# A tile's transposes in two strips of 64 rows, and new costs in the planner that orders the kernel

## The chip, the core and the metric

The kernel runs on one core of one Trainium2 chip. The metric is device time in microseconds (us). A core has a tensor engine (TensorE; its matmuls are PE in the profile, its weight loads PEld), a vector engine (DVE), a scalar engine (ACT) and a queue engine that issues transfers (SP). All of them run their own instruction streams in order and wait for each other through semaphores.

## What is computed

The input x has 4 batches of 11456 tokens with 128 channels. Everything is float32.

```python
def mab(q, kv):
    s = scale * (q @ kv.transpose(0, 2, 1))
    s = s - s.max(-1, keepdims=True)
    a = np.exp(s)
    a /= a.sum(-1, keepdims=True) + 1e-09
    return a @ kv
h = mab(I, x)          # 32 inducing points attend to all tokens of a batch
out = mab(x, h)        # every token attends to the 32 results
# then a mixture of 8 experts with one expert for each token:
# h1 = relu(tok @ w1[e]); y = h1 @ w2[e]; out = gate * sigmoid(tok @ w_output_gate[e]) * y
```

With these inputs all tokens of a batch take one expert, so the kernel loads one w1 and one w2 for each batch and folds them into 32 values for each batch; a slow path for other inputs stands behind a flag and is not taken here.

## The kernel before

A batch is cut into 6 chunks: five of 16 x 128 tokens and one of 12 x 128 (n = 16 or 12). There are 24 chunks. Each chunk passes three stages, written as generators:

- `attend_in` loads the chunk (L164, SP queue) with tokens on the partitions, transposes it on TensorE so that channels lie on the partitions (L174, one transpose for each of the n slices of 128 tokens), has ACT or DVE bring the result from PSUM to the tile xT (`bring`, L218 on ACT and L220 on DVE), computes scores (L150, four column groups of 32), a maximum (L188, L192, L195, L198), the exponential (L201), and the weighted sum h (L211, L213).
- `weigh` needs the batch's result h and xT: scores again (L150), then L478, L481, L486 on DVE and the exponential L494 on ACT.
- `attend_out`, for pairs of chunks: gates (L513, weights of 128 rows by 128 columns), a chain of small operations, and for each chunk the output matmuls (L530: for each slice four tiles of 32 rows, each into a bank of its own), scaled by DVE or ACT (`scaled`, L545 and L550) into ob or xT and written out (L571, SP queue).

Between the batch's `attend_in` and its `weigh` stand `finish` (L264, L266), `choose` (L284, and the loads of w1 and w2 issued by ACT at L304 and L310), `gates` (L344, L361) and `values` (L375, L400, L406); `known` (L423, L432, L461) is a check at the end of a batch.

A planner, `interleave`, orders all of it when the kernel is built. Each generator yields steps with an engine, a cost in us, what must be done before, and slots that it takes (8 PSUM banks among them). The planner always takes the step with the earliest start by these costs, and of equal starts the lowest key (chunk number; weigh +5, outputs +10). The order that it finds is the order on every engine. A step's result counts as done its cost plus a lag after its start:

```python
RINGS = {"bank": 8, "c": 4, "xT": 10, "p1": 2, "s2": 2, "pT": 8, "in": 4, "out": 3, "ob": 3, "w1": 1}
LAG = {"T": 0.2, "V": 0.17, "A": 0.17, "G": 0.15, "D": 1.9, "W": 1.9}
BIAS = {"T": 0.0, "V": 0.25, "A": 0.0, "G": 0.0, "D": 0.0, "W": 0.0}
```

T is TensorE, V is DVE, A is ACT, D is the transfers of SP. The costs only set the order; what a step takes on the chip is what it takes.

Of the kernel before, what the change touches and what calls it, by code (L numbers as in the profile page):

```python
# [17 lines left out]
PSUM = bass.MemoryType.PSUM  # L18

P = 128  # L20
EPS = 1e-9
CH = 16
G = 4
# [8 lines left out]
Step = namedtuple("Step", "engine cost after take give post", defaults=((), (), (), None))  # L32
# [3 lines left out]
def body(ctx: ExitStack, tc: tile.TileContext, x, inducing, w_gate, w_out_gate, w1, w2, out):  # L36
    nc = tc.nc
    B, N, C = x.shape
    M = inducing.shape[0]
    E, _, F = w1.shape  # L40
    NF = F // P
    scale = 1.0 / math.sqrt(C)
# [4 lines left out]
    while row < N:  # L47
        n = min(CH, -(-(N - row) // (G * P)) * G)
        first = min(row, N - n * P)
        chunks.append((first, n, row - first))  # L50
        row = first + n * P
    nk = len(chunks)
# [9 lines left out]
    def bank(slot, shape, dtype=F32):  # L62
        return ps.tile(shape, dtype, name="bank", tag=f"bank{slot[1]}")

    def large(slot, shape, dtype=F32):
        return xp.tile(shape, dtype, name=slot[0], tag=f"{slot[0]}{slot[1]}")

    def small(slot, name, shape, dtype=F32):
        return sp.tile(shape, dtype, name=name, tag=f"{name}{slot[1]}")


    ident = const.tile([P, P], F32, name="ident")
    make_identity(nc, ident)
    ones = const.tile([P, P], F32, name="ones")
    nc.vector.memset(ones, 1.0)
# [70 lines left out]
    def scores(s, xT, w, n):  # L146

        for g in range(G):
            r = slice(g * M, (g + 1) * M)
            nc.tensor.matmul(s[r, 0:n, :], w, xT[:, 0:n, r], start=True, stop=True)  # L150

    def attend_in(b, k):

        first, n, dup = chunks[k]
        if ("nb", b) not in st:
            st["nb", b] = gp.tile([P, nk], F32, name="nb")
            st["ha", b] = gp.tile([P, nk, C + 1], F32, name="ha")
        after = (("h", b - 2),) if b > 1 else ()
        (cslot, slot) = yield Step("D", 0.182 * n, after, (("c", 1), ("in", 1)))
        xc = large(cslot, [P, CH, C])  # L160
        src = x[b, first : first + n * P, :].rearrange("(p q) c -> p q c", q=n)
        for q in range(0, n, n if b or k else G):
            part = slice(q, q + (n if b or k else G))
            nc.sync.dma_start(xc[:, part, :], src[:, part, :])  # L164
        (tslot,) = yield Step("T", 0.0, take=(("xT", 1),))
        xT = large(tslot, [P, CH, P])
        st["xT", b, k] = xT, tslot
        for a0 in range(0, n // G, 2):
            parts = range(a0, min(a0 + 2, n // G))
            bslots = yield Step("T", 0.49 * len(parts), take=(("bank", len(parts)),))  # L170
            for a, bslot in zip(parts, bslots):
                t = bank(bslot, [P, G, P])
                for j in range(G):
                    nc.tensor.transpose(t[:, j, :], xc[:, a * G + j, :], ident)  # L174
                yield (bring(xT[:, a * G : (a + 1) * G, :], t, bslot, ("t", b, k, a)),)
        (bslot,) = yield Step("T", 0.06 * n, [("t", b, k, a) for a in range(n // G)], (("bank", 1),))
        s = bank(bslot, [P, CH, M])
        scores(s, xT, indT, n)
        if dup:

            yield Step("V", 0.5)
            full, rest = divmod(dup, n)
            nc.vector.memset(s[0:M, 0:n, 0:full], LOW)
            if rest:
                nc.vector.memset(s[0:M, 0:rest, full], LOW)
        yield Step("V", 0.06 + 0.04 * n)
        cm = small(slot, "cm", [P, 1])
        nc.vector.tensor_reduce(cm, s[:, 0:n, :], AX.XY, ALU.max)  # L188

        yield Step("V", 0.22)  # L190
        cg = small(slot, "cg", [P, G])
        nc.vector.tensor_scalar(cg, own_s, cm, None, ALU.mult)  # L192
        (mslot,) = yield Step("T", 0.25, take=(("bank", 1),))
        mb = bank(mslot, [P, 512])
        nc.tensor.matmul(mb[:, 0:G], same_m, cg, start=True, stop=True)  # L195
        nb = st["nb", b][:, k : k + 1]
        yield Step("V", 0.15, give=(mslot,))
        nc.vector.tensor_reduce(nb, mb[:, 0:G], AX.X, ALU.min)  # L198
        (pslot,) = yield Step("A", 0.46 + 0.027 * n, take=(("p1", 1),), give=(bslot,))
        p1T = small(pslot, "p1T", [P, CH, M])  # L200
        nc.scalar.activation(  # L201
            p1T[:, 0:n, :], s[:, 0:n, :], AF.Exp, bias=nb, scale=scale, accum_out=st["ha", b][:, k, C:]
        )
        yield Step("V", 0.06 + 0.04 * n)
        p1 = small(pslot, "p1", [P, CH, M])
        nc.vector.transpose(p1[:, 0:n, :], p1T[:, 0:n, :])  # L206
        (bslot,) = yield Step("T", 0.06 * n, take=(("bank", 1),), give=(cslot, pslot))
        h = bank(bslot, [P, C])
        for q in range(n):
            r = slice((q % G) * M, (q % G + 1) * M)  # L210
            nc.tensor.matmul(h[r, :], p1[:, q, :], xc[:, q, :], start=q < G, stop=q >= n - G)  # L211
        yield Step("A", 0.27, give=(bslot, slot), post=("in", b, k))
        nc.scalar.copy(st["ha", b][:, k, 0:C], h)  # L213

    def bring(dst, src, bslot, post):
        (e,) = yield Step(("A", "V"), (0.59, 0.69), give=(bslot,), post=post)
        if e == "A":
            nc.scalar.copy(dst, src)  # L218
        else:
            nc.vector.tensor_copy(dst, src)  # L220
# [20 lines left out]
    def finish(b):  # L241
# [26 lines left out]
        rl = sp.tile([P, M], F32, name="rl")  # L268
        nc.vector.tensor_scalar(rl, hb[:, 1, :], EPS, None, ALU.add)
        yield Step("V", 0.35)  # L270
# [229 lines left out]
    def attend_out(b, i):  # L500

        ks = pairs[i]
        nas = [chunks[k][1] // G for k in ks]
        n = G * sum(nas)
        lslot, slot = yield Step(
            "T", 0.24 * sum(nas), [("p", b, k) for k in ks] + [("gates", b)], (("bank", 1), ("out", 1))
        )
        p = [st.pop(("p", b, k)) for k in ks]
        L = bank(lslot, [P, 2 * CH, NG])
        t = 0  # L510
        for (pT, _), na in zip(p, nas):
            for a in range(na):
                nc.tensor.matmul(  # L513
                    L[:, t : t + G, :], pT[:, a * P : (a + 1) * P], st["gb", b], start=True, stop=True
                )
                t += G
        sm = small(slot, "sm", [P, 2 * CH])
        yield (gate(L, lslot, b, i, n, slot, sm),)
        t = 0
        for (pT, pslot), na, k in zip(p, nas, ks):  # L520

            (oslot,) = yield Step("T", 0.0, take=(("xT" if b == B - 1 else "ob", 1),))
            ob = large(oslot, [P, G, CH // G, C])
            yslots = yield Step("T", 0.1 + 0.44 * na, (("V", b), ("sm", b, i)), (("bank", G),), (pslot,))

            y = [bank(s, [P, CH // G, C]) for s in yslots]
            for a in range(na):
                for g in range(G):
                    r = slice(g * M, (g + 1) * M)
                    nc.tensor.matmul(  # L530
                        y[g][:, a, :], pT[r, a * P : (a + 1) * P], st["vb", b][r], start=True, stop=True
                    )
            for g in range(G):
                sv = sm[:, t : t + na * G].rearrange("p (a g) -> p g a", g=G)[:, g]
                yield (scaled(b, k, g, y[g], yslots[g], ob, oslot, sv, (slot,) if k == ks[-1] else ()),)
            t += na * G
# [38 lines left out]
    def gate(L, lslot, b, i, n, slot, sm):  # L575

        yield Step("V", 0.15)
        r = small(slot, "r", [P, 2 * CH])
        nc.vector.tensor_scalar(r[:, 0:n], L[:, 0:n, E + 1], EPS, None, ALU.add)
        yield Step("V", 0.35)  # L580
# [13 lines left out]
        yield Step("V", 0.18)  # L594
        nc.vector.scalar_tensor_tensor(se[:, 0:n], se[:, 0:n], EPS, r[:, 0:n], ALU.add, ALU.mult)
        yield Step("V", 0.18)
# [11 lines left out]
    for b in range(B):  # L608
        for k in range(nk):
            i = b * nk + k  # L610
# [3 lines left out]
        i = b * nk + KEY_FINISH  # L614
# [10 lines left out]
    def route(b, xv, n, gb):  # L625
# [33 lines left out]
        r = small(("out", 0), "r", [P, 2 * CH])  # L659
        nc.vector.tensor_scalar(r[0:K, 0:n], L[0:K, 0:n, 2 * E], EPS, None, ALU.add)  # L660
        nc.vector.reciprocal(r[0:K, 0:n], r[0:K, 0:n])
# [30 lines left out]
        nc.vector.tensor_reduce(u[0:K, 0, 0:n], ex[0:K, 0:n], AX.X, ALU.add)  # L692
        nc.vector.tensor_scalar(u[0:K, 0, 0:n], u[0:K, 0, 0:n], EPS, None, ALU.add)
        nc.vector.tensor_scalar(u[0:K, 1, 0:n], u[0:K, 1, 0:n], 1.0, None, ALU.add)
# [126 lines left out]
```

## Time and profile before

| | us |
|---|---|
| median of 3 timed runs | 237.44 |
| lowest, highest | 236.74, 239.01 |
| the profiled execution, own time | 235.64 |
| its span, first to last instruction | 233.9 |
| PE busy (pipelined records, so no peak) | 197.2 |
| DVE busy | 175.0 |
| ACT busy | 130.8 |

A line of the profile names the source line and engine, the output tile, the inputs, the shape and a count. For a matmul "128\*128 128x40" means weights of 128 rows by 128 columns and a moving operand of 128 rows by 40 columns. In a timeline, consecutive instructions of one line are merged into one row: start, time until the last of them ends, and their count.

### The profile page before, as it was taken

The page shows a single profiled execution, that of the slowest core. Times are in us where ns is not written, and L with a number is a line of the kernel's source. Part 1 is how long each engine was busy: PE and PEld are TensorE (multiplying, and loading weights), DVE is VectorE, ACT ScalarE, POOL GpSimd, SP SyncE. Part 2 cuts the span into 40 slices and gives each one's busy share as a digit, 9 for nine tenths or more (in the row PEclk, how much of TensorE's full clock was granted, in tenths as well). Part 3 has the DMA queues.
Part 4 walks back from the last instruction along what each step waited for, and adds up shares of the span by engine and source line. Part 5 has one row for each costly group of instructions (what it writes and reads, how often), then busy time and mean ns, then how long its engine had stood idle before and what let it go on. Part 6 is the DMA issues. An engine that isn't in the chain of part 4 may idle for free.

```text
span 233.9 us, 6634 instructions
## 1 busy us (share of the span) xinstructions
PE 197.2 (84%) x2641; PEld 138.4 (59%) x2642; DVE 175.0 (75%) x575; ACT 130.8 (56%) x337; POOL 0.7 (0%) x7
## 2 busy tenths in 40 slices
PE   2699999999999999569999999799997696879400
PEld 2556666664688777317777776365775523578300
DVE  2265475599899998927979888879889969979800
ACT  2246556538468767605658794947646716447500
POOL 1000000000000000000000000000000000000000
PEclk9999999999999999959999999999999979976955
DMA  5934576756243899990338799990017687005983
GB/s 186 381 154 149 189 301 223 224 209 244 73 144 147 223 399 409 412 397 29 99 105 335 246 295 373 408 354 18 1 64 300 249 301 276 1 4 210 374 312 127
DMA packets 18081, 52.32 MB, mean 224 GB/s; under 512 B 1665, under 2 KB 3321, under 8 KB 15609
## 3 DMA queue, kind: packets, MB, share of 16 engines
q1 hardware_dynamic: 16888, 47.61, 56.0%
q10 hardware_dynamic: 1152, 4.19, 4.8%
q8 instruction: 23, 0.38, 0.7%
q14 instruction: 18, 0.14, 0.2%
HBM read 28.34 MB, written 23.46 MB: 221 GB/s over the span
## 4 chain that ended last, share of the span: by engine, by line
PE 53%; DVE 17%; DMA 16%; ACT 5%; issue 2%; SPq 1%; ACTq 0%; DVEq 0%
PE bank L150 14%; PE bank L174 14%; DMA out_dram<-ob 8%; PE bank L513 8%; PE bank L211 6%; DMA c<-in_x_dram 5%; DVE ob L545 4%; PE bank L530 4%; DMA w1t<-in_moe_w_dram 3%; DVE xT L545 2%; ACT ob L550 2%; PE bank L375 2%; PE bank L195 2%; DVE cm L188 1%; DVE dT L486 1%
## 5 line engine op out<-in xcount | busy, mean ns | idle before, releaser
L218 ACT COPY xT<-bank 128x512 f32<-128x512 f32 x70 | 38.4, 600 | 31.8 <-PE bank L174 28.4
L174 PEld LDWEIGHTS bank<-ident,c 128*128 128x128 f32 x368 | 42.5, 148 | 21.6 <-issue 10.6
L174 PE MATMUL bank<-ident,c 128*128 128x128 f32 x368 | 50.5, 287 | 4.1 <-DMA c<-in_x_dram 4.0
L550 ACT ACTIVATE ob<-bank,sm 128x128 f32<-128x128 f32 x111 | 30.5, 381 | 13.2 <-PE bank L530 12.2
L494 ACT ACTIVATE pT<-dT 128x512 f32<-128x512 f32 (+1 forms) x24 | 26.8, 1117 | 12.2 <-DVE far L486 12.1
L530 PE MATMUL bank<-vb,pT 32*128 32x128 f32 x736 | 32.8, 306 | 0.6
L530 PEld LDWEIGHTS bank<-vb,pT 32*128 32x128 f32 x736 | 27.8, 205 | 7.8 <-issue 3.0
L545 DVE TENSOR_TENSOR ob<-bank,sm 128x512 f32<-128x512 f32 (+1 forms) x43 | 26.7, 660 | 1.3 <-DMA out_dram<-ob 0.9
L150 PE MATMUL bank<-xT,hs 128*32 128x512 f32 (+1 forms) x192 | 26.4, 641 | 0.9 <-DVE hs L274 0.9
L211 PE MATMUL bank<-c,p 128*32 128x128 f32 x736 | 25.0, 275 | 2.3 <-DVE p L206 1.8
L150 PE MATMUL bank<-xT,indT 128*32 128x512 f32 (+1 forms) x192 | 25.1, 596 | 0.9 <-ACT xT L218 0.9
L513 PEld LDWEIGHTS bank<-gb,pT 128*128 128x128 f32 x184 | 21.5, 192 | 4.7 <-issue 2.4
L211 PEld LDWEIGHTS bank<-c,p 128*32 128x32 f32 x736 | 19.1, 109 | 6.8 <-DVE p L206 2.4
L513 PE MATMUL bank<-gb,pT 128*128 128x40 f32 x184 | 22.7, 283 | 0.0
L220 DVE COPY xT<-bank 128x512 f32<-128x512 f32 x22 | 15.0, 684 | 10.0 <-PE bank L174 9.8
L188 DVE TENSOR_REDUCE cm<-bank 128x1 f32<-128x512 f32 (+1 forms) x24 | 15.8, 660 | 6.7 <-PE bank L150 6.6
L201 ACT ACTIVATE p1T<-bank,nb 128x512 f32<-128x512 f32 (+1 forms) x24 | 16.3, 678 | 7.6 <-DVE nb L198 6.5
L478 DVE TRANSPOSE_TENSOR_REDUCE mx<-bank 128x16 f32<-128x512 f32 (+1 forms) x24 | 16.5, 688 | 4.9 <-PE bank L150 4.8
L481 DVE STREAM_TRANSPOSE dT<-mx 128x512 f32<-128x512 f32 (+1 forms) x24 | 16.4, 682 | 0.1
L206 DVE STREAM_TRANSPOSE p<-p1T 128x512 f32<-128x512 f32 (+1 forms) x24 | 16.2, 677 | 0.1
L486 DVE CUSTOM_DVE_ANT_0 dT<-dT,bank 128x512 f32<-128x512 f32 (+1 forms) x24 | 15.7, 653 | 0.0
L213 ACT COPY ha<-bank 128x128 f32<-128x128 f32 x24 | 6.5, 271 | 12.6 <-PE bank L211 11.9
(115 smaller groups left out, 174.9 us busy)
## 6 DMA issues: line engine op xcount, KB each, us to landing
c<-in_x_dram SPq DMA_DIRECT2D x19, 1024.0 KB, 5.0
out_dram<-ob SPq DMA_DIRECT2D x30, 512.0 KB, 7.9
out_dram<-xT SPq DMA_DIRECT2D x10, 512.0 KB, 5.8
c<-in_x_dram SPq DMA_DIRECT2D x4, 768.0 KB, 5.6
w1t<-in_moe_w_dram ACTq DMA_DIRECT2D x4, 512.0 KB
w2t<-in_moe_w_dram ACTq DMA_DIRECT2D x4, 512.0 KB, 5.7
out_dram<-ob SPq DMA_DIRECT2D x3, 384.0 KB
c<-in_x_dram SPq DMA_DIRECT2D x4, 256.0 KB, 3.6
```

Of the source, the lines that this page charges most:

```text
L150: nc.tensor.matmul(s[r, 0:n, :], w, xT[:, 0:n, r], start=True, stop=True)
L174: nc.tensor.transpose(t[:, j, :], xc[:, a * G + j, :], ident)
L188: nc.vector.tensor_reduce(cm, s[:, 0:n, :], AX.XY, ALU.max)
L211: nc.tensor.matmul(h[r, :], p1[:, q, :], xc[:, q, :], start=q < G, stop=q >= n - G)
L218: nc.scalar.copy(dst, src)
L478: nc.vector.tensor_reduce(mx[:, 0:n], s[:, 0:n, :], AX.X, ALU.max, apply_transpose=True)
L486: nc.vector.tensor_tensor_reduce(out=dT[:, 0:n, :], in0=dT[:, 0:n, :], in1=s[:, 0:n, :], scale=1.0, scalar=0.0, op0=ALU.subtract, op1=ALU. ...
L494: nc.scalar.activation(pT[:, 0 : n * M].rearrange("p (a t h) -> p h a t", a=na, h=G), dT[:, 0:n, :].rearrange("p (h a) t -> p h a t", h=G) ...
L513: nc.tensor.matmul(L[:, t : t + G, :], pT[:, a * P : (a + 1) * P], st["gb", b], start=True, stop=True)
L530: nc.tensor.matmul(y[g][:, a, :], pT[r, a * P : (a + 1) * P], st["vb", b][r], start=True, stop=True)
L545: nc.vector.tensor_tensor(out=to, in0=y[:, 0:na, :], in1=sv.unsqueeze(2).broadcast_to([P, na, C]), op=ALU.mult)
L550: nc.scalar.activation(to[:, a, :], y[:, a, :], AF.Copy, scale=sv[:, a : a + 1])
```

## The change

The transposes of a slice of 128 tokens are cut into two strips of 64 rows (64 tokens): the weights are then 64 rows by 128 columns, and the moving identity is 64 by 64. Strip 0 of eight slices goes to one bank, strip 1 to a second bank, where before each bank took four whole slices. Each bank is brought out with one copy of 128 x 512 as before, but to every second run of 64 tokens of xT. A step with only one group of four slices (the second step of the chunk with n = 12) now takes two banks and two copies of 128 x 256. The planner's cost of a step of eight transposes goes from 0.98 to 0.8 us, and that of a chunk's output matmuls from 0.1 + 0.44 na to 0.05 + 0.27 na us, where na = n / 4.

```diff
+HP = P // 2
...
         for a0 in range(0, n // G, 2):
-            parts = range(a0, min(a0 + 2, n // G))
-            bslots = yield Step("T", 0.49 * len(parts), take=(("bank", len(parts)),))
-            for a, bslot in zip(parts, bslots):
-                t = bank(bslot, [P, G, P])
-                for j in range(G):
-                    nc.tensor.transpose(t[:, j, :], xc[:, a * G + j, :], ident)
-                yield (bring(xT[:, a * G : (a + 1) * G, :], t, bslot, ("t", b, k, a)),)
-        (bslot,) = yield Step("T", 0.06 * n, [("t", b, k, a) for a in range(n // G)], (("bank", 1),))
+            na = min(2, n // G - a0)
+            bslots = yield Step("T", 0.4 * na, take=(("bank", 2),))
+
+            t = [bank(bslot, [P, 2 * G, HP]) for bslot in bslots]
+            qs = range(a0 * G, (a0 + na) * G)
+            for q in qs:
+                for j in range(2):
+                    r = slice(j * HP, (j + 1) * HP)
+                    nc.tensor.transpose(t[j][:, q - qs.start, :], xc[r, q, :], ident[r, r])
+            for j in range(2):
+                to = xT[:, qs.start : qs.stop, j * HP : (j + 1) * HP]
+                yield (bring(to, t[j][:, 0 : len(qs), :], bslots[j], ("t", b, k, a0, j)),)
+        done = [("t", b, k, a0, j) for a0 in range(0, n // G, 2) for j in range(2)]
+        (bslot,) = yield Step("T", 0.06 * n, done, (("bank", 1),))
...
-            yslots = yield Step("T", 0.1 + 0.44 * na, (("V", b), ("sm", b, i)), (("bank", G),), (pslot,))
+            yslots = yield Step("T", 0.05 + 0.27 * na, (("V", b), ("sm", b, i)), (("bank", G),), (pslot,))
```

## Rows read from the trace of the kernel before

**Rows 1.** Stretches: length, busy PE, PEld, DVE, ACT, POOL; granted clock; DMA share; GB/s.

```profile
13.00:96.00 83.00, 81.53 (x1143) 57.42 (x1136) 65.10 (x209) 51.03 (x129) 0.00 (x0) 1.00 0.63 222
96.00:102.00 6.00, 1.29 (x11) 0.82 (x14) 3.25 (x9) 3.48 (x7) 0.00 (x0) 0.71 1.03 419
106.00:172.00 66.00, 64.52 (x896) 46.18 (x894) 55.97 (x184) 45.67 (x114) 0.00 (x0) 1.00 0.55 199
172.00:208.00 36.00, 28.16 (x376) 17.98 (x371) 32.71 (x114) 18.76 (x51) 0.00 (x0) 0.95 0.53 194
```

**Rows 2.** Timeline, weight loads (PEld): start, us, line, out, inputs, shape, count.

```profile
78.53 0.29 PEld L432 LDWEIGHTS bank<-d,ones 1*128 1x128 f32 x2
...
122.35 0.19 PEld L513 LDWEIGHTS bank<-gb,pT 128*128 128x128 f32 x1
122.59 0.98 PEld L530 LDWEIGHTS bank<-vb,pT 32*128 32x128 f32 x32
123.69 0.30 PEld L195 LDWEIGHTS bank<-cg,same_m 128*128 128x128 f32 x2
124.00 0.16 PEld L150 LDWEIGHTS bank<-xT,indT 128*32 128x32 f32 x8
```

**Rows 3.** Same view: transposes and the steps that stand right beside them.

```profile
13.71 1.73 PEld L174 LDWEIGHTS bank<-ident,c 128*128 128x128 f32 x16 [1.26 <-issue]
15.41 0.30 PEld L195 LDWEIGHTS bank<-cg,same_m 128*128 128x128 f32 x2
...
27.37 0.30 PEld L195 LDWEIGHTS bank<-cg,same_m 128*128 128x128 f32 x2 [0.20 <-issue]
27.50 1.82 PEld L174 LDWEIGHTS bank<-ident,c 128*128 128x128 f32 x16
...
34.15 0.86 PEld L174 LDWEIGHTS bank<-ident,c 128*128 128x128 f32 x8 [0.62 <-issue]
35.17 0.16 PEld L211 LDWEIGHTS bank<-c,p 128*32 128x32 f32 x8 [0.17 <-DVE bank L185]
...
162.78 0.86 PEld L174 LDWEIGHTS bank<-ident,c 128*128 128x128 f32 x8 [0.62 <-issue]
163.61 0.30 PEld L195 LDWEIGHTS bank<-cg,same_m 128*128 128x128 f32 x2
163.83 1.87 PEld L513 LDWEIGHTS bank<-gb,pT 128*128 128x128 f32 x16
165.53 0.94 PEld L174 LDWEIGHTS bank<-ident,c 128*128 128x128 f32 x8
```

**Rows 4.** Groups by line and shape: busy, mean ns, idle before; then one wait.

```profile
L218 ACT COPY xT<-bank 128x512 f32<-128x512 f32 x70 | 38.4, 600 | 31.8 <-PE bank L174 28.4 <-DMA out_dram<-ob 2.3 <-DVE xT L220 0.8
...
L213 ACT COPY ha<-bank 128x128 f32<-128x128 f32 x24 | 6.5, 271 | 12.6 <-PE bank L211 11.9 <-issue 0.3
...
PEld bank L150 <- ACT xT L218: 1.7, 3, 1.1
```

**Rows 5.** Timeline of PE and DVE at the start of the span.

```profile
4.60 3.64 PE L174 MATMUL bank<-ident,c 128*128 128x128 f32 x16 [1.71 <-DMA c<-in_x_dram]
...
8.28 0.69 DVE L220 COPY xT<-bank 128x512 f32<-128x512 f32 x1 [1.01 <-PE bank L174]
...
10.35 1.97 PE L174 MATMUL bank<-ident,c 128*128 128x128 f32 x8 [2.11 <-DMA c<-in_x_dram]
12.25 1.53 PE L150 MATMUL bank<-xT,indT 128*32 128x512 f32 x8
```

**Rows 6.** Timeline of PE and ACT: the wait for batch 1's expert, and scores elsewhere.

```profile
93.83 0.35 ACTq L304 DMA_DIRECT2D w1t<-in_moe_w_dram  x1
...
101.63 1.13 PE L375 MATMUL bank<-w1t,hs 128*32 128x256 f32 x8 [3.62 <-DMA w1t<-in_moe_w_dram]
102.54 3.31 PE L150 MATMUL bank<-xT,hs 128*32 128x512 f32 x16
...
118.31 1.06 PE L150 MATMUL bank<-xT,indT 128*32 128x512 f32 x8
```

## The prediction

> **What bounds the kernel now.** I read the busy time by stretches first, then the timeline of weight loads at single steps, the groups by line, and the timeline at the places where PE stands still. In the stretches the reader is to see that PE has work nearly all the time: 81.5 of 83 us up to 96, 64.5 of 66 us from 106 to 172, at full granted clock, while DVE has 65.1 and 56.0 us [rows 1]. PE is the bound there, so an edit is worth what it takes off PE's own time, or off the few places where PE waits: the start, the 6 us from 96 to 102, and the end from 172, where DVE has 32.7 of 36 us and PE 28.2 [rows 1].
>
> **Steady transposes: worth nothing.** A transpose is a weight load of 128 columns and a matmul that moves an identity. Sixteen of them take 1.70 us to the next step's load (13.71 to 15.41), 0.106 us each; sixteen gate matmuls, which move only 40 columns, take the same 1.70 us (163.83 to 165.53) [rows 3]. So the moving columns don't set the pace; the load of 128 columns does. Nor do the rows: of two loads with one row of weights the second starts about 0.11 us behind the first (0.29 for both, 0.18 for the last, by the nearest 0.30 of L195) [rows 2]. The strips halve the rows and the moving columns, but each strip still loads 128 columns. What they can gain is that two loads run side by side, and this the output matmuls show with tiles of 32 rows: 32 loads of 128 columns in 0.98 us, 1.10 us to the next step (122.59 to 123.69), 0.11 us for each round of four [rows 2]. Two strips side by side therefore take about 0.11 us, as one whole transpose did. By the rows, 368 transposes change by 0 (0.106 to 0.11 each is at most +1.5 us). I take 0: with two tiles for four, less offset between the tiles. The other bound is that strips halve the time, -20 us; no row bears it out, and it is a rival below. The third is that the two strips' loads run one after the other, +39 us (368 x 0.106); the output matmuls speak against it.
>
> **The joints: +2.1 us.** TensorE pays when the shape of its tiles changes. Eight transposes take 0.83 us to the next step's load if L195 follows with weights of the same shape (162.78 to 163.61) and 1.02 us if L211 with column tiles does (34.15 to 35.17): 0.19 more [rows 3]. On the way in, a step behind L195 starts 0.13 us after its loads if it is a transpose (27.37 to 27.50) [rows 3] and 0.31 us if it works in column tiles (123.69 to 124.00) [rows 2]: 0.18 more. A change of rows alone costs as well: 0.24 us from the last gate load to the first output load, against 0.106 in a run [rows 2]. Transposes have now the full shape and are the neighbours of gates, L195, L264, L284, L344 and L361 with no such cost: 10 exits (the first at 15.41, the last at 163.61) and 10 entries (the first at 27.50, the last at 165.53) [rows 3]. As strips of 64 rows they pay at each: 10 x 0.19 + 10 x 0.18 = +3.7 us. A strip's last matmul moves 64 columns for 128 and leaves the array about 0.05 us sooner (half of 0.106), at these 10 exits and at 22 others: -1.6 us. Sum +2.1 us; bounds 0 (64-row strips switch freely) and +3.7 (no shorter end). No row shows 64-row strips, so I take the sum that the other two shapes give. The Trainium skill, "TensorEngine Tiling (Array Packing)", Key Properties, says that changing the tiling mode, not just the tile, drains TensorE; the 0.19 us are this case's measure of it, and without that rule the term would be the -1.6 us alone.
>
> **Bringing the tiles out: +0.4 us.** The copies are as many and as large: 128 x 512, 600 ns on ACT [rows 4]; runs of 64 elements for whole rows I cost at nothing. Before, the first of a step's two banks is full after half the step, now both are at its end, so the first copy starts about 0.44 us later. It hides behind PE's other steps, since ACT waits for transposes 28.4 us and PE for ACT's copies only 1.7 us [rows 4]. The banks are held longer and the scores behind them are late more often: I add a quarter of 1.7, with bounds 0 and 1.7. The four chunks with n = 12 pay one more copy: 2 x 381 for 600 ns (381 from a line through 271 at 128 columns and 600 at 512 [rows 4]), 0.65 us in all, hidden in ACT's idle time (51.0 busy of 83 us [rows 1]).
>
> **The order at the start: -1.4 us.** Costs decide the order, so this follows from the code. By the planner's clock chunk 0 has landed at 4.91 and chunk 1 at 8.12. Before, its two steps of 0.98 with their lags of 0.2 end at 7.27, and the later of its two copies (0.69 on DVE, lag 0.17) at 8.13: chunk 1's transposes come first by 0.01. With 0.8 they end at 6.91, the copy at 7.77, and the scores of chunk 0 come first. On the chip chunk 0's last copy is done at 8.97 (8.28 + 0.69), but PE stands in front of chunk 1's transposes until 10.35 and does the scores after them, 1.46 us to the end of their span at 13.71 [rows 3, 5]. They fit between 8.97 and 10.35. PE being full from 13 on, I take -1.4; bounds -1.5 and 0 (the place given back at the next wait for a load).
>
> **The order of the outputs: -2.0 us.** The output step's cost falls from 1.86 to 1.13 us; the trace has 1.10 [rows 2]. The planner saw 24 such steps too long by 0.73 us, so it believed PE full when it wasn't, and put outputs (key +10) behind the next batch's work. Cheaper ones should start earlier and write earlier. What that can free is the wait at 96 to 102: DMA is saturated (share 1.03), w1 is issued at 93.83 and PE starts with it at 101.63, 3.6 us idle; the clock falls (0.71 granted), and the two scores behind take 3.31 us for 2 x 1.06, 1.2 us more [rows 1, 6]. I take under half of these 4.8 us; bounds -6 (all of it and some of the idle PE after 172) and +5 (such a wait once more, in another batch). The transposes' planned 0.8 for eight is below the 0.85 that their loads need (8 x 0.106), so the new plan errs there the other way.
>
> **Sum.** 0 + 2.1 + 0.4 - 1.4 - 2.0 = -0.9 on the profiled execution's 235.64 us: 234.7. That execution is 1.8 us below the median of the timed runs, 237.44, so 236.5 is my forecast.
>
> **Rivals.**
> *The order wins.* Outputs written earlier free the whole wait for w1 (4.8 us), the start gives 1.4, the joints cost half since the new order has fewer of them (+1): 237.44 - 5.2 = 232.2, with the idle time at 172 (36 - 28.2 us) some more, 231. For it: the output cost was the planner's largest error and is now right within 0.03 us. Against it: in 149 us of the span PE is full whatever the order [rows 1].
> *The joints lose.* One mechanism, the change of shape at the strips: the new order puts transposes beside full-shape steps at all of their some 36 runs, on one side on average, 36 x 0.185 = 6.7 us less 36 x 0.05 = 1.8 for the short ends: +4.9, with the order's 1.4 at the start -1.4: 241. It decides as soon as the order's gain is under 2 us. For it: 0.18 and 0.19 us measured at both sides, on an engine that is full. Against it: most of the strips' neighbours work in column tiles, where the cost is paid already.
> *The strips halve the transposes.* Side by side at 0.053 us each, -0.053 x 344 (without the 24 at the start, which wait for loads) = -18 us: 219. DVE would allow it (18 and 10 us idle up to 172 [rows 1]). Against it: gates with 40 moving columns and loads with one row keep the pace of 0.106. The Trainium skill, "TensorEngine Tiling (Array Packing)", Theoretical Speedup, gives up to 2x where a small dimension is at most 64, and this rival is what that would be; the trace's loads speak against it.
> *Nothing moves.* Costs that rearrange little, strips at the old pace and joints mostly in column tiles: 237.4.
>
> **How the numbers follow.** Forecast 236.5: 0.32, of which 0.04 fall below and 0.03 above 1%. Order wins 0.30; strips halve 0.06; nothing moves 0.04; joints lose 0.28. A difference under 1% (235.1 to 239.8) can't be told from none here. So faster 0.04 + 0.30 + 0.06 = 0.40, same 0.25 + 0.04 = 0.29, slower 0.03 + 0.28 = 0.31. The forecast's own range, by the bounds of its smaller terms, is 233 to 239.5; for 8 in 10 it has to reach into both sides, to 229.5 (the order's bound of -6 with the start) and 242.5 (+5 with the joints' bound), leaving the halved strips out.
>
> **What would show it.** Transposes: eight pairs of strips should stand 0.85 to 0.9 us apart, start to start of neighbouring steps without a change; 0.45 would be the halving, 1.7 the loads in line. Joints: about 0.2 us between a strip and L195 or L513. Start: chunk 0's scores ahead of chunk 1's transposes, at about 9. Outputs: the first L530 and the first write earlier in the batch, and no 3.6 us before L375. I am wrong on the strips if the pace falls under 0.1 us for a pair, and on the order if PE has new waits for c, w1 or copies in place of the old.

## The result: 0.989 of the time before, with the profile after

The changed kernel takes 236.12 us at the median (20 runs, 232.16 to 241.23), the kernel before 237.75 us beside it (20 runs, 235.12 to 245.25). The ratio of after to before is 0.9887, with a 95% interval from 0.9843 to 0.993: faster by 1.1%, or 2.7 us (1.7 to 3.7 by the interval). Single runs of one program spread by some per cent here, and the ratios leave disturbed runs out, so ratios are compared below and not medians.

The profiled execution of after took 232.78 us, its span 231.0 us (before 235.64 and 233.9). Its engines were busy for (us, share of the span, instructions):

```profile
PE 191.8 (83%) x3009; PEld 132.9 (58%) x3010; DVE 176.2 (76%) x576; ACT 130.7 (57%) x346; POOL 0.7 (0%) x7
```

PE's busy time fell by 5.4 us (197.2 before). By stretches (length; busy PE, PEld, DVE, ACT, POOL; granted clock; DMA share; GB/s) it shows:

```profile
13.00:96.00 83.00, 74.95 (x1257) 49.95 (x1258) 65.13 (x207) 48.25 (x118) 0.00 (x0) 0.95 0.64 218
96.00:102.00 6.00, 6.00 (x106) 3.25 (x103) 4.81 (x17) 3.89 (x8) 0.00 (x0) 0.86 0.42 159
106.00:172.00 66.00, 61.34 (x1042) 44.82 (x1036) 59.19 (x195) 45.98 (x130) 0.00 (x0) 0.97 0.72 248
172.00:208.00 36.00, 28.98 (x323) 20.01 (x323) 27.68 (x98) 16.42 (x44) 0.00 (x0) 0.80 0.45 165
```

Against [rows 1], PE now has holes: 75.0 busy of 83 us where it had 81.5, 61.3 of 66 where it had 64.5. The instructions in a stretch are other ones, so the sums can't be set off against each other, but two things can be read: time came free on PE, and only some of it left the span; and the granted clock is lower, 0.95 for 1.00 in the first stretch, 0.80 for 0.95 in the last, so that some of PE's busy time is the old work done more slowly.

The timeline of weight loads (start, us, line, out, inputs, shape, count) has the pace of the strips:

```profile
22.29 0.19 PEld L202 LDWEIGHTS bank<-cg,same_m 128*128 128x128 f32 x1
22.50 0.58 PEld L178 LDWEIGHTS bank<-ident,c 64*128 64x128 f32 x16
23.14 0.30 PEld L202 LDWEIGHTS bank<-cg,same_m 128*128 128x128 f32 x2
23.46 0.58 PEld L178 LDWEIGHTS bank<-ident,c 64*128 64x128 f32 x16
```

Eight pairs of strips take 0.64 us to the next step (22.50 to 23.14); eight whole transposes took 0.83 beside a full-shape step and 1.02 beside column tiles [rows 3]. The forecast was 0.85 to 0.9. From L202 to the strips behind it 0.32 us pass (23.14 to 23.46), where a whole transpose came after 0.13 [rows 3].

The groups of the copies (out, in, shapes, count, then busy and mean ns, then idle before them):

```profile
L225 ACT COPY xT<-bank 128x512 f32<-128x512 f32 x63 | 35.1, 607 | 18.9 <-PE bank L178 18.8
L225 ACT COPY xT<-bank 128x256 f32<-128x256 f32 x7 | 2.3, 380 | 0.6 <-PE bank L178 0.5
```

607 ns for 600 [rows 4], although the copy writes runs of 64 elements; 380 ns at 256 columns, as estimated.

### The profile page after: what moved, and what is told of

It is laid out like the page before. It is cut to its first block, busy times and chain, and to the rows that moved or that the text cites. A ratio compares the mean times of both kernels' runs of the same rounds, so it can differ in the third digit from the quotient of the medians.

```text
span 231.0 us, 7377 instructions
## 1 busy us (share of the span) xinstructions
PE 191.8 (83%) x3009; PEld 132.9 (58%) x3010; DVE 176.2 (76%) x576; ACT 130.7 (57%) x346; POOL 0.7 (0%) x7
## 3 DMA queue, kind: packets, MB, share of 16 engines
HBM read 28.34 MB, written 23.46 MB: 224 GB/s over the span
## 5 line engine op out<-in xcount | busy, mean ns | idle before, releaser
L225 ACT COPY xT<-bank 128x512 f32<-128x512 f32 (+1 forms) x70 | 37.4, 585 | 19.5 <-PE bank L178 19.3
L178 PEld LDWEIGHTS bank<-ident,c 64*128 64x128 f32 x736 | 29.1, 150 | 20.8 <-issue 7.7
L178 PE MATMUL bank<-ident,c 64*128 64x64 f32 x736 | 35.0, 242 | 6.1 <-DMA c<-in_x_dram 4.1
L537 PE MATMUL bank<-vb,pT 32*128 32x128 f32 x736 | 34.3, 321 | 0.2
L537 PEld LDWEIGHTS bank<-vb,pT 32*128 32x128 f32 x736 | 29.4, 219 | 8.7 <-issue 2.3
L218 PE MATMUL bank<-c,p 128*32 128x128 f32 x736 | 25.8, 280 | 3.5 <-DVE p L213 2.9
L151 PE MATMUL bank<-xT,indT 128*32 128x512 f32 (+1 forms) x192 | 26.7, 621 | 1.5 <-ACT xT L225 1.3
L151 PE MATMUL bank<-xT,hs 128*32 128x512 f32 (+1 forms) x192 | 27.8, 663 | 0.2 <-ACT xT L225 0.2
L520 PEld LDWEIGHTS bank<-gb,pT 128*128 128x128 f32 x184 | 24.1, 211 | 3.2 <-ACT pT L501 1.4
L520 PE MATMUL bank<-gb,pT 128*128 128x40 f32 x184 | 25.5, 302 | 0.2 <-ACT ob L557 0.2
L227 DVE COPY xT<-bank 128x512 f32<-128x512 f32 (+1 forms) x26 | 17.6, 677 | 9.5 <-PE bank L178 9.5
L218 PEld LDWEIGHTS bank<-c,p 128*32 128x32 f32 x736 | 19.7, 112 | 7.2 <-DVE p L213 2.5
L195 DVE TENSOR_REDUCE cm<-bank 128x1 f32<-128x512 f32 (+1 forms) x24 | 15.7, 654 | 4.7 <-PE bank L151 4.6
L493 DVE CUSTOM_DVE_ANT_0 dT<-dT,bank 128x512 f32<-128x512 f32 (+1 forms) x24 | 15.5, 650 | 0.0
```

The costliest lines, as they stand in the source:

```text
L178: nc.tensor.transpose(t[j][:, q - qs.start, :], xc[r, q, :], ident[r, r])
L520: nc.tensor.matmul(L[:, t : t + G, :], pT[:, a * P : (a + 1) * P], st["gb", b], start=True, stop=True)
L537: nc.tensor.matmul(y[g][:, a, :], pT[r, a * P : (a + 1) * P], st["vb", b][r], start=True, stop=True)
```

## Experiments

### What a strip costs

**m1_paces** computes nothing of the reference: it loads one chunk and times series of transposes and products on TensorE, each series behind the copy of the one before it.

```diff
+    def strips(rows):
+        k = P // rows
+        t = banks(k)
+        for i in range(32):
+            for j in range(k):
+                r = slice(j * rows, (j + 1) * rows)
+                nc.tensor.transpose(t[j][:, (i % 4) * rows : (i % 4 + 1) * rows], xc[r, i % CH, :], ident[r, r])
...
+    def one_group():
+        t = banks(1)
+        for i in range(32):
+            r = slice(0, 64)
+            nc.tensor.transpose(t[0][:, 0:64], xc[r, i % CH, :], ident[r, r])
```

> A kernel that only times TensorE: after 40 transposes that bring it to its clock, 32 whole transposes (weights 128x128), 32 pairs of strips (64x128, two banks), 32 rounds of four strips (32x128, four banks), 32 strips of one row group alone, and then plain float32 products with a moving operand of 64 columns and weights of 128, 64 and 32 rows, 16 rounds each. It computes nothing of the reference and writes one small block. Theory A, a weight load's time follows its rows where it is a strip's: about 0.107 us for a whole transpose, 0.06 for a pair of strips of 64, 0.03 to 0.06 for a round of four strips of 32; one group alone about 0.055 for each strip; plain products show the same halving, 0.06 instead of 0.107 for a pass. Theory B, the halving belongs to transposes alone: the plain products stay at 0.107 us for a pass at 64 and 32 rows, as the output matmuls did before. Theory C, the halving comes from the two groups side by side: one group alone takes 0.107 for each strip.

It took 51.72 us. Its weight loads, L65 whole transposes, L75 strips of 64 and then of 32 rows, L83 strips of 64 rows in one row group only:

```profile
11.94 3.48 PEld L65 LDWEIGHTS bank<-ident,xc 128*128 128x128 f32 x32 [0.54 <-ACT got L54]
15.90 2.22 PEld L75 LDWEIGHTS bank<-ident,xc 64*128 64x128 f32 x64 [0.48 <-ACT got L54]
18.55 2.18 PEld L75 LDWEIGHTS bank<-ident,xc 32*128 32x128 f32 x128 [0.44 <-ACT got L54]
21.16 2.73 PEld L83 LDWEIGHTS bank<-ident,xc 64*128 64x128 f32 x32 [0.42 <-ACT got L54]
```

32 whole transposes take 3.48 us, 0.109 each. 32 pairs of strips take 2.22 us, of which the first and last loads' own length is part: 0.060 to 0.066 a pair from start to start. Four strips of 32 rows side by side take as long as two of 64. One row group alone paces at 0.060 to 0.067 a strip as well (start to start over its first 18 strips; from 22.3 us on, the granted clock is 0.50), so a strip is quicker by itself, and the second one beside it costs nothing. Plain products ran at half the clock in m1, so they were measured again.

**m2_paces**, which computes nothing of the reference either, sets plain products (L80, two passes each) and transposes (L69) of several sizes between series of whole transposes, so that all of it runs at one clock.

```diff
+        turn(128, 24)
+        multiply(64, 64, 8)
+        turn(128, 24)
+        multiply(32, 64, 8)
+        turn(128, 24)
+        multiply(128, 64, 8)
+        turn(128, 24)
+        turn(96, 24)
+        turn(128, 24)
+        turn(64, 24)
```

> A second kernel that only times TensorE and computes nothing of the reference: plain float32 products with a moving operand of 64 columns and weights of 64, 32 and 128 rows, each short and behind a run of whole transposes so that the clock stays up, and then transposes of 96 rows and of 64. Theory A (a transposed tile's pace is set by its moving columns, one for each row transposed; its weight load is faster than a plain product's): 96 rows take 0.08 us each, three quarters of 0.107, and plain products take 0.107 for a pass at 128, 64 and 32 rows alike. Theory B (the load sets it, and is faster only in tiles of 64 rows or fewer): 96 rows take 0.107, as the whole; plain products as in A or halved as well.

It took 48.65 us. Its weight loads:

```profile
16.62 1.97 PEld L80 LDWEIGHTS bank<-ident,xc 64*128 64x128 f32 x32 [0.48 <-ACT got L54]
22.06 1.98 PEld L80 LDWEIGHTS bank<-ident,xc 32*128 32x128 f32 x64 [0.49 <-ACT got L54]
27.51 1.86 PEld L80 LDWEIGHTS bank<-ident,xc 128*128 128x128 f32 x16 [0.49 <-ACT got L54]
...
32.84 2.05 PEld L69 LDWEIGHTS bank<-ident,xc 96*128 96x128 f32 x24 [0.49 <-ACT got L54]
35.35 2.61 PEld L69 LDWEIGHTS bank<-ident,xc 128*128 128x128 f32 x24 [0.46 <-ACT got L54]
38.44 1.70 PEld L69 LDWEIGHTS bank<-ident,xc 64*128 64x128 f32 x48 [0.49 <-ACT got L54]
```

A plain product that moves 64 columns paces at 0.11 us a round, whether a round is one load of 128 rows, two of 64 or four of 32 (16 rounds in 1.86 to 1.98 us). A transpose paces at 0.109, 0.083 and 0.060 to 0.066 us for 128, 96 and 64 rows, which are as many moving columns. So two paces that look alike were taken for one limit: that of a plain product, about 0.11 us whatever its rows, and that of a whole transpose, about 0.109 us, which falls with the transpose's size. A strip's load of 128 columns takes at most the 0.06 us of the strip. Since a transpose has as many rows as moving columns, these runs can't tell which of the two sets its pace; that the rows make no difference to plain products speaks for the columns.

### Strips and order apart

**e1_strips_old_costs** has the strips and the planner's costs of before. (The order isn't quite that of before: the last step of a chunk with n = 12 takes two banks.)

```diff
-            bslots = yield Step("T", 0.4 * na, take=(("bank", 2),))
+            bslots = yield Step("T", 0.49 * na, take=(("bank", 2),))
...
-            yslots = yield Step("T", 0.05 + 0.27 * na, (("V", b), ("sm", b, i)), (("bank", G),), (pslot,))
+            yslots = yield Step("T", 0.1 + 0.44 * na, (("V", b), ("sm", b, i)), (("bank", G),), (pslot,))
```

> The strips alone: the planner keeps the costs of before (0.49 for four transposes, 0.1 + 0.44 na for outputs), so the order is nearly that of before. The strips take some 17 us off TensorE. Theory A (TensorE was the bound in that order, the gain is lost in the new order): 224 to 230 us. Theory B (the gain is lost in any order, since DVE, the loads and a lower clock take TensorE's place): 234 to 238 us.

235.37 us, before 239.51 in the same session; ratio 0.9864 [0.9744, 0.9984]. About 3 us (237.75 x 0.0136; 0.4 to 6 by the interval) for some 17 us less of transposes. In the profiled execution (span 233.4 us, 233.9 before) PE is busy 10.1 us less than the 197.2 of before, and idle 9.6 us more (46.3 for 36.7):

```profile
PE 187.1 (80%) x3009; PEld 128.7 (55%) x3010; DVE 178.0 (76%) x584; ACT 126.8 (54%) x330; POOL 0.7 (0%) x7
```

One of the waits can be read in one chunk's cycle, in the timeline (start, us, engine, line, out, inputs, shape, count, idle before). Before:

```profile
19.95 1.06 PE L150 MATMUL bank<-xT,indT 128*32 128x512 f32 x8
...
20.94 1.09 PE L174 MATMUL bank<-ident,c 128*128 128x128 f32 x8
21.08 0.69 DVE L188 TENSOR_REDUCE cm<-bank 128x1 f32<-128x512 f32 x1 [0.86 <-PE bank L150]
...
21.69 0.70 DVE L206 STREAM_TRANSPOSE p<-p1T 128x512 f32<-128x512 f32 x1
...
22.45 1.08 PE L211 MATMUL bank<-c,p 128*32 128x128 f32 x32 [0.41 <-DVE p L206]
...
23.77 1.06 PE L150 MATMUL bank<-xT,indT 128*32 128x512 f32 x8
```

And e1, the same steps:

```profile
19.44 1.06 PE L151 MATMUL bank<-xT,indT 128*32 128x512 f32 x8
...
20.44 0.71 PE L178 MATMUL bank<-ident,c 64*128 64x64 f32 x16
20.57 0.69 DVE L195 TENSOR_REDUCE cm<-bank 128x1 f32<-128x512 f32 x1 [0.86 <-PE bank L151]
21.18 0.70 DVE L213 STREAM_TRANSPOSE p<-p1T 128x512 f32<-128x512 f32 x1
...
21.94 1.08 PE L218 MATMUL bank<-c,p 128*32 128x128 f32 x32 [0.79 <-DVE p L213]
...
23.26 1.06 PE L151 MATMUL bank<-xT,indT 128*32 128x512 f32 x8
```

The eight transposes take 0.38 us less (1.09 to 0.71), and PE's wait for DVE's p grows by 0.38 us (0.41 to 0.79). Scores to scores is 3.82 us in both. In this cycle the path goes scores, maximum, transposition of the earlier chunk's p, its h, through DVE; PE's transposes stood beside it. Over the whole span such waits are the smaller part: PE's idle time before h (L211, then L218) and the maximum's product (L195, then L202) rises from 2.5 to 4.2 us. The larger part goes to transfers, as the waits show (engine, line waited for; us, times, longest), first before, then e1:

```profile
PE bank L174 <- DMA c<-in_x_dram: 4.0, 3, 2.1
PE bank L375 <- DMA w1t<-in_moe_w_dram: 3.6, 1, 3.6
```

```profile
PE bank L178 <- DMA c<-in_x_dram: 9.4, 5, 3.2
PE bank L382 <- DMA w1t<-in_moe_w_dram: 6.1, 2, 3.7
```

5.4 us more for chunks and 2.5 us more for w1: 7.9 of the 9.6 us.

**e2_whole_new_out_cost** has the whole transposes and the cost 0.49 of before, with the new cost of the outputs alone. Against before:

```diff
-            yslots = yield Step("T", 0.1 + 0.44 * na, (("V", b), ("sm", b, i)), (("bank", G),), (pslot,))
+            yslots = yield Step("T", 0.05 + 0.27 * na, (("V", b), ("sm", b, i)), (("bank", G),), (pslot,))
```

> The order alone: whole transposes as before at 0.49, and only the planner's cost of the outputs at 0.05 + 0.27 na. Theory A (the new order is the loss): 240 to 246 us. Theory B (the order's share is small): 234 to 239. My prediction's term for it was -2.0 on 237.4: 235.4.

240.39 us beside 239.51 of before in the session; six runs give no interval. No gain is seen, and a loss isn't shown.

**e3_whole_new_costs** has the whole transposes with both new costs. Against before, beside e2's line:

```diff
-            bslots = yield Step("T", 0.49 * len(parts), take=(("bank", len(parts)),))
+            bslots = yield Step("T", 0.4 * len(parts), take=(("bank", len(parts)),))
```

> Whole transposes as before, with both of the planner's new costs (0.4 for four transposes, 0.05 + 0.27 na for outputs): an order near that of the changed kernel, with the transposes at their old time, some 17 us more on TensorE. Theory A (the strips bring their time, the order costs it): 244 to 252. Theory B (TensorE's time isn't the bound in the new order): 236 to 240.

244.75 us; ratio 1.0206 [1.0082, 1.033]: the new costs without the strips lose 4.9 us (237.75 x 0.0206). With after's ratio the strips in this order (nearly: the last step of a chunk with n = 12 takes one bank here) are worth 1.0206 - 0.9887 = 0.032, or 7.6 us, give or take 3 by the two intervals; in nearly the old order 3.2.

**e5_strips_twice** is after with each strip transposed twice into the same place.

```diff
-                for j in range(2):
+                for j in (0, 1, 0, 1):
                     r = slice(j * HP, (j + 1) * HP)
```

> The changed kernel with each strip transposed twice, the same result written again: the planner's costs and with them the order stay, and TensorE gets back about 0.06 x 368 = 23 us of work. Theory A (in this order TensorE's time is on the path all along): +15 to +23 us, 250 us or more. Theory B (chains through DVE, ACT and the loads set most of the time and TensorE waits in them): +3 to +10 us, 239 to 246.

247.79 us, before 238.2; ratio 1.0576 [1.0366, 1.0785]. 368 pairs more at 0.062 us are 23 us of PE; the ratio rose by 0.069 over after's, or 16 us, give or take 5 by the two intervals. So added PE time stands for the most part on the path in this order. The share (about 70%) looks larger than that of the time taken away (7.6 of 17), but with these intervals a difference between the two isn't shown.

**e7_shorter_cost** tells the planner the measured pace of the strips.

```diff
-            bslots = yield Step("T", 0.4 * na, take=(("bank", 2),))
+            bslots = yield Step("T", 0.33 * na, take=(("bank", 2),))
```

> The changed kernel with the planner's cost of a transpose step at 0.33 for four slices (0.66 for eight), which is what eight pairs of strips took in the trace of the changed kernel (0.64 to 0.68 us to the next step where that follows at once); 0.4 there. Only the order differs. Theory A (the more exact the costs, the better the order): 1 to 3 us less than the changed kernel, 233 to 235. Theory B (each order has waits of its own, whatever its costs): anywhere within 4 us on either side, no gain from the exactness.

235.41 us, before 239.69; ratio 0.9934 [0.9856, 1.0011], not to be told from after's 0.9887. The truer cost brings no gain that can be seen.

### What holds the changed kernel

**e6_half_max** takes the maximum over half of the scores (the other half is left out), to shorten DVE's part of the cycle.

```diff
-        nc.vector.tensor_reduce(cm, s[:, 0:n, :], AX.XY, ALU.max)
+        nc.vector.tensor_reduce(cm, s[:, 0 : n // 2, :], AX.XY, ALU.max)
```

> The changed kernel, with the maximum that shifts the first exponential (cm) taken over half of the scores: it leaves out the other half. The order stays. It takes 24 x 0.33 = 8 us off DVE, each time in the chain scores, maximum, exponential, transposition, weighted sum of a chunk. Theory A (TensorE is the bound): within 1 us of the changed kernel. Theory B (that chain and DVE are the bound): -3 to -8 us, 228 to 233.

234.57 us, before 238.2; ratio 0.996 [0.9855, 1.0065]. No gain over after. In single profiled executions DVE's busy time fell from 176.2 to 170.6 us, and the part from the first batch's `finish` to the last one's took 135.4 us for 138.3; in the total it can't be found. DVE's maximum alone, which stood on the path in the stretch shown of e1, isn't what holds after's order.

**e9_fill_gates** puts 24 transposes of the identity, whose result nobody reads, ahead of the last batch's gate product, where after's PE stands idle and runs at the lower clock.

```diff
+        if b == B - 1:
+            for _ in range(24):
+                nc.tensor.transpose(gd[:, 0:P], ident, ident)
```

> The changed kernel with 24 idle transposes put into TensorE's wait ahead of the last batch's gates matmul (2.9 us idle there in the profiled execution), into the bank that this matmul then overwrites; the order of all else stays. Theory A (the lower granted clock behind that wait costs time: the gate matmuls of the first pair took 3.64 us for 1.9 in front of w1's matmul): the clock stays up behind it and the time falls by 1 to 2.5 us. Theory B (the lower clock there is hidden by DVE's work): no change, or up to +0.5 us.

The PE timeline there, first of after, then of e9:

```profile
188.90 0.39 PE L351 MATMUL bank<-wd,h 128*128 128x9 f32 x2 [2.55 <-DVE wd L348]
189.22 1.39 PE L151 MATMUL bank<-xT,hs 128*32 128x512 f32 x8
190.54 3.64 PE L520 MATMUL bank<-gb,pT 128*128 128x40 f32 x16
194.11 1.13 PE L382 MATMUL bank<-w1t,hs 128*32 128x256 f32 x8
```

```profile
187.63 2.84 PE L353 MATMUL bank<-ident 128*128 128x128 f32 x24
190.31 0.29 PE L354 MATMUL bank<-wd,h 128*128 128x9 f32 x2
190.53 1.07 PE L151 MATMUL bank<-xT,hs 128*32 128x512 f32 x8
191.69 1.95 PE L523 MATMUL bank<-gb,pT 128*128 128x40 f32 x16
193.57 1.11 PE L385 MATMUL bank<-w1t,hs 128*32 128x256 f32 x8
```

The same 16 gates take 3.64 us in after, at a granted clock of 0.50 (1.2 GHz), after PE had waited 2.55 us for wd, and 1.95 in e9, at 1.00 (2.4 GHz), behind the idle transposes and the scores. The mean granted clock is 0.904 to 0.931 in e9's runs, 0.872 to 0.905 in after's. But the time is 233.75 us, before 238.2; ratio 0.9963 [0.9874, 1.0052]: no gain over after's 0.9887. The lower clock at this place costs the total nothing that can be seen; what it costs elsewhere stays open.

**e8_c5** gives the chunks and their loads a fifth slot.

```diff
-RINGS = {"bank": 8, "c": 4, "xT": 10, "p1": 2, "s2": 2, "pT": 8, "in": 4, "out": 3, "ob": 3, "w1": 1}
+RINGS = {"bank": 8, "c": 5, "xT": 10, "p1": 2, "s2": 2, "pT": 8, "in": 5, "out": 3, "ob": 3, "w1": 1}
```

> The changed kernel with five slots for loaded chunks (c and in) where it has four; loads can be issued a chunk earlier, and the planner's order follows. Theory A (behind TensorE, the loads and their slots set the pace): 3 to 6 us less, 230 to 233. Theory B (they don't; the chain of a chunk through DVE and ACT and TensorE's remaining work do): 235 to 239.

226.0 us (225.38 to 228.04), before 239.69; ratio 0.9616 [0.9452, 0.9779]: faster than both kernels, with intervals that don't meet. Its engines, and the first stretch:

```profile
PE 191.2 (86%) x3009; PEld 133.5 (60%) x3010; DVE 172.5 (77%) x570; ACT 135.4 (61%) x361; POOL 0.7 (0%) x7
13.00:96.00 83.00, 79.52 (x1358) 53.25 (x1358) 67.63 (x209) 54.66 (x133) 0.00 (x0) 1.00 0.65 232
```

PE has 79.5 us of work in the first 83 where after has 75.0, ACT 54.7 where it has 48.3: more of the batch's work lies there. The last chunk's load is issued at 127.2 us for 145.2 in after, and from the first `finish` to the last 128.1 us pass for 138.3. After's PE waits for chunks from 13 to 185 us add up to 1.3 us only, so most of the 6.4 us that e8 gains on after (237.75 x 0.0271) came through the order that earlier loads allow. In the profiled executions PE is busy as long (191.2 us for 191.8) and idle 6.8 us less (32.4 for 39.2): its idle time before h (L218), `choose` (L291) and `gates` (L351), most of it waits for DVE, falls from 9.3 to 1.7 us. Whether whole transposes with five slots gain as much wasn't tried; how much of it the strips made possible stays open.

**e10_fill_half** is e6 and e9 together, and **e11_c5_fill_half** both with five slots (half of the scores are left out of the maximum in both).

```diff
-        nc.vector.tensor_reduce(cm, s[:, 0:n, :], AX.XY, ALU.max)
+        nc.vector.tensor_reduce(cm, s[:, 0 : n // 2, :], AX.XY, ALU.max)
...
+        if b == B - 1:
+            for _ in range(24):
+                nc.tensor.transpose(gd[:, 0:P], ident, ident)
```

> The changed kernel in its own order with two edits that leave the order alone: 24 idle transposes in TensorE's wait ahead of the last batch's gates (2.2 us off the end in the profiled execution) and the first exponential's shift from half of the scores (2.9 us off the middle); it leaves out the other half in that maximum. If the two gains are real and add up: 3 to 5 us less than the changed kernel, 231 to 233 us by the median. If they were the spread of single executions: 235 to 237.

> The same two edits with five slots for loaded chunks, in the order that the planner finds for them; it leaves out half of the scores in the first maximum. If the slots are the bound behind TensorE: 228 to 231 us. If not: as the two edits alone, give or take 4 us for another order.

e10: 235.0 us (226.69 to 241.62), no interval, inconclusive. e11: 227.44 us, ratio 0.9572 [0.9346, 0.9797], not to be told from e8's 0.9616. No gain from the maximum or from the clock at that place is seen, with four slots or with five.

## Why the prediction was right and wrong

The point, 236.5, is 0.4 us from the median of after, and the sign is right, but the number stood on two errors that nearly cancelled: PE lost far more work than it said, and work taken off PE was worth far less than it said. By the ratios, both new costs with whole transposes are +4.9 us (e3) and the strips in that order -7.6 (after against e3), -2.7 in all; the forecast had -3.4 for the order and +2.5 for the strips with their joints and copies. So that the point was met is luck.

**Steady transposes: the term was mis-sized, 0 for some -17 us of PE.** The step that failed is the first one: "the moving columns don't set the pace; the load of 128 columns does", read off gates that move 40 columns and keep the same 0.106 us [rows 3]. For transposes that doesn't hold: plain products keep 0.11 us a round at any number of rows (m2), transposes take 0.109 us at 128 rows and moving columns and 0.063 at 64 (m1, m2). Equal times of two kinds of instruction were taken for one cause. That two strips run side by side, read off the output matmuls [rows 2], held: a pair paces like one strip alone. The rival that had the halving got a chance of 0.06; its pace of 0.053 was near the measured 0.063, its gain of 18 us was not. The Trainium skill, "TensorEngine Tiling (Array Packing)", Theoretical Speedup, gives up to 2x for a dimension of at most 64, and the trace agrees: 0.109 / 0.063 = 1.7. It holds for transposes here and not for plain products, which take 0.11 us for one load of 128 rows and for two of 64.

**The bound: "an edit is worth what it takes off PE's own time" failed.** That step read 81.5 busy of 83 us as a full engine [rows 1]. The halving rival multiplied by it too, and so came to 219. With 17 us off PE's transposes the time fell by 3.2 us in nearly the old order (e1) and 7.6 us in the new (after against e3). In e1 most of what left PE came back as waits for chunks and w1, 7.9 us, and a smaller part as waits for DVE: the wait of 0.41 us before h stood in the trace of before already, in front of L211, in a cycle of 3.82 us that ran through DVE. I had read where PE stood still for long, not which loads and which chains stood close behind it.

In after the waits are another matter: they are about as long as before (PE idle 39.2 us for 36.7), and its transposes' rows fell by 15.5 us (50.5 to 35.0), but PE's busy time by 5.4 only. The rows of the transposes, before and after (busy, mean ns, idle before):

```profile
L174 PE MATMUL bank<-ident,c 128*128 128x128 f32 x368 | 50.5, 287 | 4.1 <-DMA c<-in_x_dram 4.0
L178 PE MATMUL bank<-ident,c 64*128 64x64 f32 x736 | 35.0, 242 | 6.1 <-DMA c<-in_x_dram 4.1
```

More of the other work ran at the lower clock. These are the sums over all stretches at a granted clock of 0.50 (1.2 GHz), of before and then of after (length, busy PE, PEld, DVE, ACT, POOL):

```profile
sum 29.40, PE 13.88 PEld 7.96 DVE 9.72 ACT 4.62 POOL 0.00; mean PE 3.47 PEld 1.99 DVE 2.43 ACT 1.15 POOL 0.00
sum 48.00, PE 35.55 PEld 24.16 DVE 25.37 ACT 22.36 POOL 0.00; mean PE 5.08 PEld 3.45 DVE 3.62 ACT 3.19 POOL 0.00
```

The same 16 gates took 3.64 us at that clock in after and 1.95 at the full one in e9, so about half of the 21.7 us more, some 11 us, is the same work done more slowly (an estimate). That doesn't make the clock the cause of the small gain: in e9 the clock was higher and the time no shorter.

**Joints: the prices were right, the count was not.** Eight pairs to the next step of another shape take 0.64 us; 8 x 0.0625 = 0.50 leaves 0.14, and 0.19 - 0.05 had been forecast. Entries take 0.315 us behind L202 in 7 of 9 cases, where whole transposes took 0.136: 0.18 more, as forecast. In after's order strips stand behind a full-shape step 14 times and ahead of one 15 times, for the 10 and 10 counted. What the joints cost in the total wasn't measured by itself.

**Copies: right.** 607 for 600 ns, and 380 for 381 estimated at 256 columns.

**The start: the order was right, the gain can't be shown.** Chunk 0's scores now stand ahead of chunk 1's transposes:

```profile
5.06 2.58 PE L178 MATMUL bank<-ident,c 64*128 64x64 f32 x32 [2.20 <-DMA c<-in_x_dram]
8.30 2.06 PE L151 MATMUL bank<-xT,indT 128*32 128x512 f32 x8 [0.67 <-ACT xT L225]
10.94 1.78 PE L178 MATMUL bank<-ident,c 64*128 64x64 f32 x32 [0.57 <-DMA c<-in_x_dram]
```

At 8.30, for 9 forecast. They take 2.06 us, twice the later 1.06, and the strips beside them are as slow (2.58 us for 16 pairs), although the granted clock is 1.00 in the records there; that wasn't settled. The first batch's `finish` starts at 40.1 us in after, at 44.4 in before, and at 42.4 in e9, whose steps are the same up to there: 1.4 us can't be told from such differences.

**The outputs' order: with the start's -1.4, the -2.0 us was wrong in sign for the two costs together.** The wait for w1 fell as hoped, from 3.6 us [rows 6] to this:

```profile
PE bank L382 <- DMA w1t<-in_moe_w_dram: 0.9, 1, 0.9
```

But the first output matmul starts at 75.70 us, not earlier than before (73.36), and e3 shows that both new costs with whole transposes lose 4.9 us. The transposes' cost of 0.4, below what whole ones take, has part in e3; e2, with the outputs' cost alone, shows no gain and can't tell more. With strips the new costs are about even with the old ones: 0.9887 against 0.9864, with intervals that overlap. One wait that goes is no measure of an order: other places change with it.

**The base.** The sum stood on 235.64 us and the forecast added back the 1.8 us to the median; before's median over 20 runs, 237.75, is close to the 237.44 that this took. Chances: "faster by over 1%" got 0.40, the most of the three, for the order's sake; the time went that way by the strips, and by 1.1%, with an interval that reaches down to 0.7%.

## What to carry to other kernels

An instruction's pace is read from a run of the same kind at two sizes; that another kind takes as long says nothing of the cause. A busy share near 1 on PE doesn't mean that all the time taken off it is won: look for what stands close behind it, the loads and the short waits inside one cycle of the loop, before pricing work taken off, and set PE's busy time against its idle time and its granted clock afterwards. A planner's better costs are a new order and are to be timed by themselves, as is one more slot for what is loaded ahead: here that was worth more than the change.

## What the runs showed of the hardware

A transpose with weights of 128 columns paces at 0.109, 0.083 and 0.063 us for 128, 96 and 64 moving columns (some 0.85 ns a column at 128 and 96, about 1 ns at 64), and strips of 32 rows, four to a round, at 0.064: below 64 rows nothing more is won. A plain product in these forms keeps 0.11 us a round at 128, 64 and 32 rows. And less work for TensorE in the same order went with a lower clock: the mean granted clock is 0.872 to 0.905 in after's runs, 0.911 to 0.924 in e5's with the strips done twice, and 0.904 to 0.931 in e9's with 24 idle transposes. The order matters too: of the profiled executions' spans, 48.0 us of after's are at 1.2 GHz, 29.5 of before's, 35.1 of e1's and 39.6 of e8's.
